# Superblocks 1 and 2 of a fused convolution and squared-ReLU network: casts on ScalarE, maxima a pair a step, 16-bit copies a superblock later

## The chip, the cores and the metric

The kernel runs on one core of one Trainium2 chip. The metric is the device time of one execution in microseconds (us); before the change it is 2076.97 us, the median of three runs (2076.81 to 2077.22).

The core has five instruction queues that run side by side and wait for each other by semaphores: TensorE (PE, its weight loads as PEld), VectorE (DVE), ScalarE (ACT), GpSimd (POOL) and SyncE (SP, which here issues nearly all DMAs). Each queue works strictly in its own order: an instruction that waits holds back all behind it.

## The reference

A causal convolution over seven taps whose weights are a softmax per head, and behind it a two-layer network with the square of a ReLU:

```python
def _attn_ref(x, weight):                    # x: 8 x 4096 x 192, weight: 8 heads x 7 taps
    ...
    w = np.exp(weight - np.max(weight, axis=-1, keepdims=True))
    w = w / (np.sum(w, axis=-1, keepdims=True) + 1e-09)
    ...
    out = np.einsum('hk,bskhg->bshg', w, x_unf)
    return out.reshape(B, S, D).astype(np.float32)

def _moe_ref(x, w_in, w_out, s, b):          # x: 32768 x 192, 2048 hidden columns
    h = x @ w_in
    r = np.maximum(h, 0.0)
    g = s * (r * r) + b
    return (g @ w_out).astype(np.float32)
```

## The kernel before, in words

**Tiling.** The 32768 tokens are cut into 32 superblocks of 1024, and each of these into two blocks j of 512. The 2048 hidden columns are cut into eight pairs p of two chunks of 128. The main loop (from line 981 on) runs over the steps (n, j, p): superblock, block, pair. Superblock 0 has its own code; the loop begins at n = 1. A step calls `first(n, j, p)`: 18 multiplications that put hidden columns of the block into a PSUM tile h (two such tiles exist). ScalarE takes `relu` of h into q and squares q in place. `square` then casts q to a rounded copy qh, and `lows` (or `half_lows` from n = 3 on) subtracts qh from q on VectorE, which gives the low part ql: every factor is split into a high and a low part, so that products of reduced precision add up to full precision. Each step is put into `queue`, and `second(n, j, p, qh, ql)`, which multiplies with the output weights into four accumulators, follows at least two steps later (`LAG = 2`); a block's first pair is held one step longer, since the accumulators must first be evicted by ScalarE (lines 809 and 812) and summed by GpSimd (813, 817, 822). In that place two `first` stand together and then two `second`.

**Tokens.** Superblock n + 1 is convolved during superblock n, a tap at a time: the class `Tokens` holds the work as a generator of 28 steps, first seven taps into accA for block 0 and its split into sA, then seven taps into accB (the last 64 features of both blocks) and its split into tB, then accA for block 1. `convolve(k)` does the next k taps on VectorE, behind what VectorE and ScalarE had been given before. What a call couldn't do, because a part ended, is owed to the next. After a split, `swap` copies sA to wA and tB to wB with the two halves of the partitions exchanged: two DMAs on SyncE each. `first` of the new superblock reads sA, then tB and wB, then wA.

**Scales.** From superblock 3 on ql is 16-bit, and tokens are scaled by powers of two. For that `peak()` takes the maxima of the tokens two superblocks ahead, at step (n, 1, 3). `to_all` sends them to a DRAM tile "there" and back to all partitions as a tile t: two DMAs on SyncE, of which the second waits for the first. `scale()` uses t at step (n, 1, 7). The weights have scales too: `weight_tops` and `weight_peaks` take their maxima in block (2, 0), `weight_scales` computes g, c and c8 with a few small operations on VectorE and GpSimd, `rescale(p)` multiplies the output weights of pair p by g on ScalarE after their last use in superblock 2, and `halve(p)` makes 16-bit copies of their high parts for the products with the 16-bit ql. `biases()` in step (2, 0, 0) computes what b adds to the output and adds it to the three blocks that had been kept back in the output buffers.

**Order.** Instructions are recorded in the order of the code, and a scheduler orders them per engine; `behind(...)` keeps a piece of work behind what an engine had last. DMAs of later loads (xA, xB) are often issued a superblock before the place in the code that asks for them. The words used below: "there" and "t" are the two DMAs of `to_all`, "peak" the two reductions on line 207.

Of the kernel before, what the change touches and what calls it, by code (L numbers as in the profile page):

```python
# [9 lines left out]
F32 = mybir.dt.float32  # L10
# [4 lines left out]
AF = mybir.ActivationFunctionType  # L15
# [18 lines left out]
SCALED = 3  # L34
# [10 lines left out]
def conv_attention_then_squared_relu_mlp(  # L45
# [23 lines left out]
    nc = tc.nc  # L69
    D, T = outT.shape  # L70
    NPAIR = weights64.shape[0]
    K = taps.shape[2]
    PAD = K - 1
    DB = D - P
# [47 lines left out]
    def behind(*engines):  # L122
        return last_of(*engines)()
# [34 lines left out]
    def greatest(wide, count):  # L158

        out = small.tile([P, 2], F32, name="m")[:, 0:count]  # L160
        nc.vector.tensor_reduce(
            out, wide.rearrange("p (c k) -> p c k", c=count), axis=AX.X, op=ALU.max
        )
        return out

    def powers(of, power, other, low):

        nc.vector.tensor_scalar(of, of, 2.0**low, 2.0**60, op0=ALU.max, op1=ALU.min)
        of, power, other = (v.bitcast(I32) for v in (of, power, other))
        nc.vector.tensor_scalar(power, of, EXPONENT, None, op0=ALU.bitwise_and)  # L170
        nc.vector.tensor_scalar(
            other, of, EXPONENT, EXPONENT, op0=ALU.bitwise_and, op1=ALU.bitwise_xor
        )

    g, c, undo, c8 = (scales[:, k : k + 1] for k in range(4))
# [173 lines left out]
    WB = wide_w.tile([P, NPAIR, 2, 2 * DB], F32R, name="WB")  # L349
# [231 lines left out]
    def weight_tops(p):  # L581

        for to, w in (
            (tops[:, p : p + 1], W[:, p, 0, 0:CI]),
            (tops[:, NPAIR + p : NPAIR + p + 1], W[:, p, 0, CI:CB]),
            (tops[:, 2 * NPAIR + p : 2 * NPAIR + p + 1], WB[:, p, :, 0:DB]),
        ):
            nc.vector.tensor_reduce(  # L588
                to, w.bitcast(F32), axis=AX.XY if w.shape[1] == 2 else AX.X, op=ALU.max,
                apply_absolute_value=True,  # L590
            )

    def weight_peaks():

        for k, some in enumerate((tops[:, 0:NPAIR], tops[:, NPAIR:])):
            nc.vector.tensor_reduce(both_tops[:, k : k + 1], some, axis=AX.X, op=ALU.max)
        return to_all(both_tops)

    def weight_scales(wide):

        m = greatest(wide, 2)
        power, other = scales[:, 4:6], scales[:, 6:8]
        powers(m, power, other, -30)
        nc.gpsimd.tensor_scalar(c, other[:, 0:1], 0.5, None, op0=ALU.mult)
        nc.gpsimd.tensor_scalar(c8, other[:, 0:1], 2.0**2, None, op0=ALU.mult)
        nc.gpsimd.tensor_scalar(g, other[:, 1:2], 2.0**3, None, op0=ALU.mult)
        nc.gpsimd.tensor_tensor(undo, power[:, 0:1], power[:, 0:1], op=ALU.mult)
        nc.gpsimd.tensor_scalar(undo, undo, power[:, 1:2], 2.0**-12, op0=ALU.mult, op1=ALU.mult)
        nc.gpsimd.tensor_scalar(undo, undo, sb, None, op0=ALU.mult)

    halves = []

    def halve(p):

        if not halves:
            free = wordp.tile([P, CT, 2], I32, name="words").bitcast(F16)
            free = free.rearrange("p f w -> p (f w)")
            halves.append(free[:, 0 : NF * P].rearrange("p (f c) -> p f c", f=NF))
            halves.append(free[:, NF * P : NF * (P + DB)].rearrange("p (f c) -> p f c", f=NF))
        f = slice(2 * p, 2 * p + 2)  # L620
        a = W[:, p, 0, CI:CB].bitcast(F32).rearrange("p (f c) -> p f c", f=2)
        nc.scalar.activation(halves[0][:, f, :], a, AF.Identity, scale=g)
        nc.scalar.activation(
            halves[1][:, f, :], WB[:, p, :, 0:DB].bitcast(F32), AF.Identity, scale=g
        )

    def rescale(p):

# [23 lines left out]
    def first(n, j, p, meanwhile=None):  # L652
        h = ps_h.tile([P, 2, BLK], F32, name="h")
        halves = [tok[n].half(j, i) for i in range(2)]

        def both(w, part, at, start, stop):

            for i in range(2):
                chunk = halves[i][at]
                rows = slice(i * HB, (i + 1) * HB)  # L660
                nc.tensor.matmul(  # L661
                    h[:, i, :], w_in(w, p, chunk[0], rows), folded(chunk[part]),
                    start=start, stop=stop,
                )

        for at in (0, 2, 1):
            both(0, 1, at, at == 0, False)
            both(0, 2, at, False, False)
            both(1, 1, at, False, at == 1)
            if meanwhile and at == 0:  # L670
                meanwhile()
        return h

    def relu(h, scale=1.0):
        q = act.tile([P, 2, BLK], F32, name="q")
        nc.scalar.activation(q, h, AF.Relu, scale=scale)  # L676
        return q

    def squares(h, cast, scale=1.0):
        return square(relu(h, scale), cast)  # L680

    def square(q, cast):
        nc.scalar.activation(q, q, AF.Square)  # L683
        qh = qs.tile([P, 2, BLK], F32R, name="qh")
        cast(qh, q)  # L685
        return q, qh

    def lows(q, qh):
        ql = qs.tile([P, 2, BLK], F32R, name="ql")
        nc.vector.tensor_tensor(ql, q, qh.bitcast(F32), op=ALU.subtract)  # L690
        return qh, ql
# [188 lines left out]
    def load_tokens(n):  # L880
        if n < NSUP:
            ahead[n] = Tokens(n)
            ahead[n].load()

    def start_tokens(n):
        if n < NSUP:
            if n not in ahead:
                load_tokens(n)
            tok[n] = ahead.pop(n)
# [7 lines left out]
    def convolve(k):  # L897


        k += owed[0]  # L900
        with behind(nc.vector, nc.scalar):
            while k and coming[0] in tok:
                try:
                    stop = next(tok[coming[0]].todo)
                except StopIteration:
                    coming[0] += 1
                    continue
                k -= 1
                if stop:
                    break  # L910
        owed[0] = k if coming[0] in tok else 0
# [54 lines left out]
    for n, j, p in steps:  # L966
        if p == 0:
            tok[n].finish(j)
            if j == 0:
                with headed():  # L970
                    start_tokens(n + 1)
            else:
                tok.pop(n - 1)
                if n >= SCALED:
                    tok[n].unscale()
                    tok_s[n] = tok[n].s
        if j == 1 and SCALED <= n + 2 < NSUP:
            if p == 0:
                load_tokens(n + 2)
            elif p == 3:  # L980
                with behind(nc.vector):
                    ahead[n + 2].peak()
            elif p == 7:
                with behind(nc.vector):
                    ahead[n + 2].scale()
        if n == SCALED - 1:
            if j == 1:
                halve(p)
            elif p < 4:
                with behind(nc.vector):  # L990
                    weight_tops(2 * p)
                    weight_tops(2 * p + 1)
                    if p == 3:
                        wide_tops = weight_peaks()
            elif p == 7:
                with behind(nc.vector):
                    weight_scales(wide_tops)
        with begun() if n == 1 else ExitStack():
            h = first(n, j, p)
            if n < SCALED:  # L1000
                low = lows(*squares(h, nc.vector.tensor_copy))
            else:
                low = half_lows(n, j, p, *squares(h, nc.vector.tensor_copy, c if n == SCALED else 1.0))
            queue.append((n, j, p, *low))
        if (n, j) == (1, 1):
            if p < NPAIR - 1:
                with behind(nc.vector):
                    column_sums(p + 1)
            convolve(1)
        elif p < NPAIR - 1 or n == 1:  # L1010

            convolve(3 if n == 1 else 3 - p % 2 if n == 2 else 2)
        if (n, j, p) == (2, 0, 0):
            biases()


        while queue and len(queue) > LAG + (queue[0][2] == 0 and queue[0][:2] != (1, 0)):
            item = queue.pop(0)
            (second if item[0] else second_whole)(*item)
# [47 lines left out]
```

## Time and profile before

| | |
|---|---|
| median of three runs | 2076.97 us |
| the profiled execution | 2077.24 us |
| its span, first to last instruction | 2075.5 us |
| PE / DVE / ACT / POOL busy | 99% / 89% / 63% / 21% |
| granted TensorE clock | 1.00 |

The page gives each engine's busy time over the span. Beside it three views are used. The view of stretches gives each engine's busy time between two moments. The timeline gives instructions in the order of time, with the idle time before one and what ended it in square brackets. The view of groups collects instructions of one line and shape: count, busy time, the mean of one in ns, and after the bar the idle time before them. The wait view says who waited for whom: us in total, times, longest.

### The profile page before, as it was taken

Reading aid. Unit: us, or ns where it says so; the run is one execution under the profiler, and the core shown is the slowest. Engines: PE = TensorE matmul, PEld = TensorE weight load, DVE = VectorE, ACT = ScalarE, POOL = GpSimd, SP = SyncE. Lnnn points to the kernel's source line nnn. Section 1 sums busy time; section 2 is a strip of 40 time slices with the busy share of each in tenths; the row PEclk is TensorE's granted clock in tenths of the full one; section 3 lists DMA queues with packets and bytes.
Section 4 is the critical chain, followed back from the end, with each engine's and each line's share of the span. In section 5 each row is a group of like instructions: output and inputs, shape, how many; then the busy total and the mean of one; then the engine's idle time right before and its main releaser. Section 6 shows DMA issues by size and latency. Waiting matters only on the chain.

```text
span 2075.5 us, 43142 instructions
## 1 busy us (share of the span) xinstructions
PE 2052.6 (99%) x18404; PEld 1593.7 (77%) x18404; DVE 1842.3 (89%) x2201; ACT 1298.3 (63%) x1440; POOL 429.6 (21%) x298
## 2 busy tenths in 40 slices
PE   9998999999999999999999999999999999999999
PEld 6786777777777777777777777777777777777776
DVE  9998899889988889988899898899888899888975
ACT  8855765666666656656666656666666566566665
POOL 0014221212211212212212112122112122122210
PEclk9999999999999999999999999999999999999999
DMA  5012221212221222221122212222212222221210
GB/s 193 21 50 68 59 60 48 64 50 68 59 60 47 57 57 63 62 56 54 52 62 60 59 48 61 53 69 57 62 47 57 57 62 62 56 55 44 54 42 19
DMA packets 58640, 121.35 MB, mean 58 GB/s; under 512 B 16400, under 2 KB 20496, under 8 KB 58448
## 3 DMA queue, kind: packets, MB, share of 16 engines
q1 hardware_dynamic: 58304, 118.47, 21.0%
q8 instruction: 144, 2.36, 0.5%
q14 instruction: 48, 0.39, 0.1%
q10 hardware_dynamic: 144, 0.13, 0.0%
HBM read 35.57 MB, written 25.20 MB: 29 GB/s over the span
## 4 chain that ended last, share of the span: by engine, by line
PE 91%; DVE 6%; ACT 1%; issue 1%; DMA 0%; POOL 0%; SPq 0%; DVEq 0%; ACTq 0%
PE h L661 45%; PE acc L773 30%; PE acc L792 10%; PE acc L758 5%; DVE ql L690 1%; DVE accA L239 1%; DVE qh L685 1%; DVE c L405 0%; DVE t L391 0%; ACT q L676 0%; DVE tops L588 0%; ACT q L683 0%; DVE W L411 0%; DVE words L571 0%; DVE t L388 0%
## 5 line engine op out<-in xcount | busy, mean ns | idle before, releaser
L676 ACT ACTIVATE q<-h 128x1024 f32<-128x1024 f32 x496 | 506.5, 1021 | 638.7 <-PE h L661 637.1
L703 DVE TENSOR_TENSOR ql<-q,qh 128x1024 f16<-128x1024 f32 x464 | 584.9, 1261 | 24.7 <-PE acc L773 0.9
L683 ACT ACTIVATE q<-q 128x1024 f32<-128x1024 f32 x512 | 542.0, 1059 | 14.2
L773 PE MATMUL acc<-qh,W 64*128 64x512 f32 x3960 | 515.1, 376 | 0.2
L685 DVE CAST qh<-q 128x1024 fp32r<-128x1024 f32 x497 | 349.8, 704 | 167.4 <-ACT q L683 163.9
L661 PE MATMUL h<-sA,W 64*128 64x512 f32 x3072 | 488.3, 423 | 4.7 <-ACT q L676 2.9
L773 PEld LDWEIGHTS acc<-qh,W 64*128 64x128 f32 x3960 | 376.2, 186 | 53.2 <-ACT oA L812 0.8
L661 PE MATMUL h<-wA,W 64*128 64x512 f32 x3072 | 416.1, 376 | 0.0
L661 PE MATMUL h<-wB,W 64*128 64x512 f32 x1536 | 413.8, 376 | 1.3 <-DMA wB<-tB 1.3
L661 PE MATMUL h<-tB,W 64*128 64x512 f32 x1536 | 413.7, 376 | 0.0
L661 PEld LDWEIGHTS h<-sA,W 64*128 64x128 f32 x3072 | 286.5, 186 | 100.8 <-ACT oA L809 23.5
L239 DVE SCALAR_TENSOR_TENSOR accA<-xA,taps,accA 128x512 f32<-128x512 f32 x348 | 341.9, 983 | 6.2
L661 PEld LDWEIGHTS h<-wA,W 64*128 64x128 f32 x3072 | 291.5, 186 | 40.8
L773 PE MATMUL acc<-qh,WB 64*128 64x512 f32 x1980 | 312.9, 388 | 4.4 <-DVE qh L685 2.3
L661 PEld LDWEIGHTS h<-tB,W 64*128 64x128 f32 x1536 | 285.0, 186 | 27.2 <-issue 0.2
L661 PEld LDWEIGHTS h<-wB,W 64*128 64x128 f32 x1536 | 285.0, 186 | 15.6 <-DMA wB<-tB 2.0
L792 PE MATMUL acc<-ql,words 64*128 64x512 f16 x1852 | 280.6, 382 | 0.0
L817 POOL TENSOR_TENSOR oA<-oA,oA 128x512 f32<-128x512 f32 x61 | 111.1, 1821 | 808.0 <-ACT oA L812 808.0
L773 PEld LDWEIGHTS acc<-qh,WB 64*128 64x128 f32 x1980 | 188.9, 186 | 37.9 <-DVE qh L685 3.7
L792 PEld LDWEIGHTS <-words 64*128 64x128 f16 x1852 | 53.8, 95 | 111.0 <-issue 111.0
L239 DVE SCALAR_TENSOR_TENSOR accB<-xB,taps,accB 128x512 f32<-128x512 f32 x174 | 131.2, 754 | 3.1
L822 POOL TENSOR_TENSOR oC<-oC,oB 64x512 f32<-64x512 f32 x60 | 95.9, 1599 | 147.9 <-DMA oC<-oB 140.2
(152 smaller groups left out, 1397.9 us busy)
## 6 DMA issues: line engine op xcount, KB each, us to landing
wA<-sA SPq DMA_DIRECT2D x126, 256.0 KB, 3.7
outT<-oA SPq DMA_DIRECT2D x63, 256.0 KB, 2.0
wB<-tB SPq DMA_DIRECT2D x60, 256.0 KB, 3.2
xA<-in_xA SPq DMA_DIRECT2D x24, 515.0 KB, 4.4
xB<-in_xB SPq DMA_DIRECT2D x32, 259.0 KB, 2.6
oC<-oB SPq DMA_DIRECT2D x61, 128.0 KB, 2.2
outT<-oC SPq DMA_DIRECT2D x60, 128.0 KB, 2.3
words<-in_w SPq DMA_DIRECT2D x7, 768.0 KB, 6.4
```

The lines of the kernel that those rows point to most:

```text
L239: nc.vector.scalar_tensor_tensor(acc, src, w[:, k : k + 1], acc, op0=ALU.mult, op1=ALU.add)
L661: nc.tensor.matmul(h[:, i, :], w_in(w, p, chunk[0], rows), folded(chunk[part]), start=start, stop=stop,)
L676: nc.scalar.activation(q, h, AF.Relu, scale=scale)
L683: nc.scalar.activation(q, q, AF.Square)
L685: cast(qh, q)
L690: nc.vector.tensor_tensor(ql, q, qh.bitcast(F32), op=ALU.subtract)
L703: nc.vector.tensor_tensor(ql.rearrange("p f (b a) -> p f b a", a=2), *(v.rearrange("p f (a b) -> p f b a", a=2) for v in (q, qh.bitcast(F3 ...
L758: nc.tensor.matmul(to[k * DB :][0:DB], halves[1][:, 2 * p + k, :], ql[:, k, :], start=False, stop=p == NPAIR - 1, skip_group_check=True,)
L773: nc.tensor.matmul(accs[to + 2 * i], w(f, r), folded(q[r, f % 2, :]), start=start and f == 0, stop=stop and f == ends[i],)
L792: nc.tensor.matmul(accs[2 * i], halves[0][r, f, :], ql[r, f % 2, :], start=False, stop=f == ends[i],)
L817: nc.gpsimd.tensor_tensor(o[0], o[0], o[2], op=ALU.add)
L822: nc.gpsimd.tensor_tensor(oB, oC, o[1][0:DB], op=ALU.add)
```

## The change

It has five parts. (1) In superblocks 1 and 2 the casts of block (1, 0), of block (2, 0) and of the odd pairs of block (1, 1) run on ScalarE, 20 in all; the others stay on VectorE. (2) The weights' maxima are taken for one pair in each of the eight steps of block (2, 0), and no longer for two pairs in each of its first four. (3) So `weight_peaks` moves from step (2, 0, 3) to (2, 0, 7), and `weight_scales` from (2, 0, 7) to (2, 1, 3). (4) `halve` moves from block (2, 1) to block (3, 0); by then the weights carry g already, so that it copies without a factor. (5) In superblock 2 `convolve` gets two taps after each step, no longer three and two by turns.

```diff
-        nc.scalar.activation(halves[0][:, f, :], a, AF.Identity, scale=g)
-        nc.scalar.activation(
-            halves[1][:, f, :], WB[:, p, :, 0:DB].bitcast(F32), AF.Identity, scale=g
-        )
+        nc.scalar.copy(halves[0][:, f, :], a)
+        nc.scalar.copy(halves[1][:, f, :], WB[:, p, :, 0:DB].bitcast(F32))
...
         if n == SCALED - 1:
-            if j == 1:
-                halve(p)
-            elif p < 4:
+            if j == 0:
                 with behind(nc.vector):
-                    weight_tops(2 * p)
-                    weight_tops(2 * p + 1)
-                    if p == 3:
+                    weight_tops(p)
+                    if p == NPAIR - 1:
                         wide_tops = weight_peaks()
-            elif p == 7:
+            elif p == 3:
                 with behind(nc.vector):
                     weight_scales(wide_tops)
+        elif (n, j) == (SCALED, 0):
+            halve(p)
         with begun() if n == 1 else ExitStack():
             h = first(n, j, p)
             if n < SCALED:
-                low = lows(*squares(h, nc.vector.tensor_copy))
+                on_scalar = (n, j) in ((1, 0), (2, 0)) or (n, j, p % 2) == (1, 1, 1)
+                low = lows(*squares(h, nc.scalar.copy if on_scalar else nc.vector.tensor_copy))
...
-            convolve(3 if n == 1 else 3 - p % 2 if n == 2 else 2)
+            convolve(3 if n == 1 else 2)
```

What this does to the order shows at three places. First VectorE in block (3, 1), whose order repeats in every later superblock; qh is a step's cast, ql its subtraction, accB the taps, tB and hiB the split, peak the maxima two superblocks ahead. Before, from the split after the subtraction of (3, 1, 1):

```order
L267 CAST hiB<-accB 128x512
L271 CAST tB<-accB 64x512
L272 TENSOR_TENSOR tB<-accB,hiB 64x512
L685 CAST qh<-q 128x1024
L703 TENSOR_TENSOR ql<-q,qh 128x1024
L271 CAST tB<-accB 64x512
L272 TENSOR_TENSOR tB<-accB,hiB 64x512
L237 TENSOR_SCALAR accA<-xA,taps 128x512
L207 TENSOR_REDUCE peak<-xA 128x1
L207 TENSOR_REDUCE peak<-xB 128x1
L685 CAST qh<-q 128x1024
L703 TENSOR_TENSOR ql<-q,qh 128x1024
```

Now, from the cast of (3, 1, 2):

```order
L683 CAST qh<-q 128x1024
L701 TENSOR_TENSOR ql<-q,qh 128x1024
L239 SCALAR_TENSOR_TENSOR accB<-xB,taps,accB 128x512 x2
L207 TENSOR_REDUCE peak<-xA 128x1
L207 TENSOR_REDUCE peak<-xB 128x1
L683 CAST qh<-q 128x1024
L701 TENSOR_TENSOR ql<-q,qh 128x1024
L239 SCALAR_TENSOR_TENSOR accB<-xB,taps,accB 128x512
L683 CAST qh<-q 128x1024
L701 TENSOR_TENSOR ql<-q,qh 128x1024
L267 CAST hiB<-accB 128x512
L271 CAST tB<-accB 64x512
```

The split of accB stood ahead of the maxima and stands behind them now, after the subtraction of (3, 1, 4).

Second SyncE's DMAs at the same place: outputs of the block before, the swap of tB into wB, the two DMAs of the maxima, loads. Before:

```order
L821 DMA outT<-oA 128x512
L816 DMA oC<-oB 64x512
L826 DMA outT<-oC 64x512
L248 DMA wB<-tB 64x1024
L247 DMA wB<-tB 64x1024
L151 DMA there<-peak 128x2x1
L153 DMA t<-there 128x256
L198 DMA xA<-in_xA 128x1030
```

Now:

```order
L819 DMA outT<-oA 128x512
L814 DMA oC<-oB 64x512
L824 DMA outT<-oC 64x512
L151 DMA there<-peak 128x2x1
L153 DMA t<-there 128x256
L195 DMA xB<-in_xB 128x518
L248 DMA wB<-tB 64x1024
L247 DMA wB<-tB 64x1024
L198 DMA xA<-in_xA 128x1030
```

The two DMAs that write wB have moved behind "there", "t" and a load of xB (which before stood further ahead).

Third ScalarE in block (2, 1); words are the 16-bit copies, W and WB the output weights, scales holds g. Before, around the relus of (2, 1, 0) and (2, 1, 1):

```order
L622 ACTIVATE words<-W,scales 128x256
L623 ACTIVATE words<-WB,scales 128x128
L622 ACTIVATE words<-W,scales 128x256
L676 ACTIVATE q<-h 128x1024
L623 ACTIVATE words<-WB,scales 128x128
L683 ACTIVATE q<-q 128x1024
```

Now, around the relu of (2, 1, 4) and the one after it:

```order
L628 ACTIVATE W<-W,scales 128x2x256
L622 CAST words<-W 128x256
L674 ACTIVATE q<-h 128x1024
L681 ACTIVATE q<-q 128x1024
L628 ACTIVATE WB<-WB,scales 128x256
L623 CAST words<-WB 128x128
L628 ACTIVATE W<-W,scales 128x2x256
L622 CAST words<-W 128x256
L674 ACTIVATE q<-h 128x1024
L681 ACTIVATE q<-q 128x1024
```

The copies stood ahead of the block's second relu and waited for the scales; each pair's copies now stand beside its rescaling.

## The prediction

> Below, "step (n,j,p)" is superblock n (from 0), block j, hidden pair p; "the second superblock" is n = 1, "the third" n = 2. My forecast: **slower, 2169 us**. The change wins back some 14 us in n = 1 and n = 2, and then pays about 3.9 us at 27 later superblock borders.
>
> **What bounds the kernel now.** I read the page first, then a table of stretches of the run, then TensorE's own timeline and its waits.
>
> ```profile
> span 2075.5 us, 43142 instructions
> PE 2052.6 (99%) x18404; PEld 1593.7 (77%) x18404; DVE 1842.3 (89%) x2201; ACT 1298.3 (63%) x1440; POOL 429.6 (21%) x298
> ...
> 120.52:154.43 33.91, 33.13 (x308) 28.62 (x305) 32.81 (x44) 18.79 (x21) 5.46 (x3) 1.00 0.14 38
> 154.43:196.27 41.84, 35.56 (x315) 29.38 (x312) 39.69 (x71) 18.31 (x22) 19.80 (x12) 1.00 0.27 77
> 196.27:238.23 41.96, 35.71 (x306) 28.35 (x304) 30.96 (x41) 29.84 (x48) 6.06 (x10) 1.00 0.21 50
> 238.23:2012.00 1773.77, 1773.77 (x16212) 1374.29 (x16210) 1595.88 (x1853) 1101.78 (x1193) 387.81 (x259) 1.00 0.21 57
> ```
>
> The columns of the last four rows are the stretch, its length, then busy time of PE, PEld, DVE, ACT and POOL, the granted clock, DMA share and GB/s. From 238 us on TensorE is never idle: there is nothing to gain there, and every new wait of TensorE is paid in full. The time that can be won lies before 238 us. How much, I take from the starts of steps:
>
> ```profile
> 116.42 0.38 PE L661 MATMUL h<-sA,W 64*128 64x512 f32 x2
> 120.52 0.38 PE L661 MATMUL h<-sA,W 64*128 64x512 f32 x2
> 154.43 0.38 PE L661 MATMUL h<-sA,W 64*128 64x512 f32 x2
> 196.27 0.38 PE L661 MATMUL h<-sA,W 64*128 64x512 f32 x2
> 238.23 0.38 PE L661 MATMUL h<-sA,W 64*128 64x512 f32 x2
> ...
> PE acc L773 <- DVE ql L690: 5.6, 6, 1.9
> PE acc L773 <- DVE qh L685: 2.3, 3, 0.8
> PE acc L773 <- ACT oB L809: 2.0, 1, 2.0
> PE h L661 <- DMA wB<-tB: 1.3, 2, 0.7
> ...
> L642 PE MATMUL h<-bb,words 64*128 64x1 f32 x8 | 0.5, 226 | 0.0
> ```
>
> An undisturbed step takes 120.52 - 116.42 = 4.10 us (38 multiplications in 19 side-by-side pairs, 0.216 us a pair), so eight take 32.8. The blocks (1,1), (2,0), (2,1) took 33.9, 41.8 and 42.0: 1.1, 9.0 and 9.2 too much. Block (1,0), whose first steps have no second product yet, lost about 0.9 to late ql. Together **20.2 us** are lost, of which 0.5 are the eight small products for the bias (last row), that stay. (The four rows of waits, 90 to 240 us, add up to less, because a product that waits for its operands is also drawn longer.) The 9.0 us of (2,0) I divide so: 2.0 for wB at its start (worked out in part 4), 0.5 for the bias, 3.0 for the eviction of oB (the 2.0 of its row and about 1 of slow products behind it), and the rest, 3.5, late qh and ql.
>
> **Part 1: twenty casts to ScalarE.** The prices, from rows of the first superblocks:
>
> ```profile
> L690 DVE TENSOR_TENSOR ql<-q,qh 128x1024 fp32r<-128x1024 f32 x8 | 9.8, 1225 | 0.5
> L239 DVE SCALAR_TENSOR_TENSOR accA<-xA,tap,accA 128x512 f32<-128x512 f32 x12 | 9.0, 750 | 0.3
> L685 DVE CAST qh<-q 128x1024 fp32r<-128x1024 f32 x8 | 5.5, 689 | 1.9 <-ACT q L683 1.9
> ...
> L676 ACT ACTIVATE q<-h 128x1024 f32<-128x1024 f32 x16 | 16.3, 1016 | 0.4 <-PE h L661 0.2
> L685 ACT CAST qh<-q 128x1024 fp32r<-128x1024 f32 x15 | 15.7, 1048 | 0.5
> ...
> L812 ACT ACTIVATE oB<-acc,sb 128x512 f32<-128x512 f32 x4 | 2.7, 676 | 0.0
> ```
>
> In (1,0) VectorE does per step a cast, a subtraction and three taps: 0.69 + 1.23 + 3 x 0.75 = 4.17 us against TensorE's 4.10, so it falls behind and stays behind. Without the cast it is 3.48. ScalarE then does relu, square and cast, three times about 1.03, 3.1 us a step, inside 4.10. So the late ql of n = 1 go, but for the first step, where nothing hides that ScalarE's cast is 0.36 longer: of the 2.0 us of n = 1, 0.6 stay. In (2,0) the casts (8 x 0.69) and half of each maxima step go from VectorE's worst stretch: of the 3.5 us of late qh and ql I leave 0.5. ScalarE also evicts four accumulators a block between these casts (0.68 each, last row) and casts two tiles sA as large: 8 x 3.1 + 6 x 0.68 = 28.9, still under 32.8.
>
> **Part 2: the maxima, a pair a step.** Their number stays; the bias of (2,0,0) no longer stands behind two pairs of them. VectorE being ahead too, the bias comes about 3 us sooner relative to TensorE, the GpSimd additions behind it free the output buffer sooner, and the wait for the eviction of oB (3.0 us) shrinks to about 0.7.
>
> **Part 3: the 16-bit copies a superblock later.** In (2,1) ScalarE now stands still for the scales, and then has 16 copies between its relus:
>
> ```profile
> L622 ACT ACTIVATE words<-W,scales 128x256 f16<-128x256 f32 x8 | 4.0, 496 | 6.2 <-POOL scales L606 6.2
> ```
>
> That is a wait of 6.2 us and 4.0 us of copies, their eight smaller partners on top, and TensorE's late relu, qh and ql of (2,1) follow from it. After the change the copies stand beside the rescaling, under 1 us a step, on an engine that then is busy for nearly the whole 4.10. The scales come at step 3 and their GpSimd steps behind that block's output additions; a relu is late by about 3 us there, of 4 us that the lag of two steps allows. I leave 1.0 of the 9.2 us.
>
> Still there in n = 2: the wait for wB in (2,0,0), 2.0 before and about 1.6 after (both sides move forward by 1.5 to 2 us), and a new one of about 1.4 into (3,0,0), priced like the next part. Left in all: 0.6 + 0.5 + 0.7 + 1.0 + 1.6 + 1.4 + 0.5 = 6.3. **Gain 20.2 - 6.3 = 14 us**, between 8 (half of what I call gone stays) and 18.
>
> **Part 4: where the taps now stand.** The last line of the diff (two taps a step in n = 2, not three and two by turns) looks harmless, but it shifts the taps against the steps, and the shift stays for all later superblocks. So accB's taps end after the maxima of the tokens two superblocks on (peak), not before; hence in SyncE's queue the swap of tB into wB now stands behind "there", "t" and an xB load. The trace of before has this very order once, in n = 1, and shows its price:
>
> ```profile
> 149.75 0.34 SPq L153 DMA_DIRECT2D t<-there  x1
> 150.19 0.47 SPq L248 DMA_DIRECT2D wB<-tB  x1
> ...
> 157.75 0.59 PE L661 MATMUL h<-wA,W 64*128 64x512 f32 x4
> ```
>
> "t" can't be issued before "there" has landed, and wB lands late behind the broadcast "t". The products with wA should have come 12 multiplications (1.30 us) after 154.43, at 155.73; they came at 157.75, so TensorE lost 2.02 us with "t" issued at 149.75. In other words: **loss = issue of t + 6.7 - start of the next superblock** (149.75 + 6.7 - 154.43 = 2.0).
>
> In the steady part, before the change:
>
> ```profile
> 405.97 0.38 PE L661 MATMUL h<-sA,W 64*128 64x512 f32 x2
> 425.94 0.57 PE L661 MATMUL h<-sA,W 64*128 64x512 f32 x2
> ...
> 412.40 0.55 SPq L248 DMA_DIRECT2D wB<-tB  x1
> 415.08 0.38 SPq L151 DMA_DIRECT2D there<-peak  x1
> 423.04 0.33 SPq L153 DMA_DIRECT2D t<-there  x1
> ...
> wB<-tB SPq DMA_DIRECT2D x56, 256.0 KB, 3.2
> xB<-in_xB SPq DMA_DIRECT2D x26, 259.0 KB, 2.6
> ```
>
> Step (5,1,3) starts at 405.97, superblock 6 at 425.94; wB left at 412.4, long before. "there" to "t" is 423.04 - 415.08 = 7.96 us. When does peak end after the change? By the new order it stands behind the casts and subtractions of (5,1,0) to (5,1,2) and four taps of accB:
>
> ```profile
> 403.75 1.25 DVE L703 TENSOR_TENSOR ql<-q,qh 128x1024 f16<-128x1024 f32 x1
> ...
> 407.23 1.07 ACT L683 ACTIVATE q<-q 128x1024 f32<-128x1024 f32 x1
> ...
> 404.31 1.83 POOL L817 TENSOR_TENSOR oA<-oA,oA 128x512 f32<-128x512 f32 x1 [24.30 <-ACT oA L812]
> ...
> 409.93 1.86 POOL L822 TENSOR_TENSOR oC<-oC,oB 64x512 f32<-64x512 f32 x1 [2.36 <-DMA oC<-oB]
> ...
> 373.40 3.46 DVE L239 SCALAR_TENSOR_TENSOR accA<-xA,taps,accA 128x512 f32<-128x512 f32 x2
> ...
> 413.23 1.22 DVE L207 TENSOR_REDUCE peak<-xA 128x1 f32<-128x1030 f32 x1
> 414.37 0.68 DVE L207 TENSOR_REDUCE peak<-xB 128x1 f32<-128x518 f32 x1
> ```
>
> The subtraction of (5,1,1) gives VectorE back at 404.9. Two taps beside GpSimd's additions (as at 373.40, 3.46) end at 408.3, when the square of (5,1,2) is just done. Cast and subtraction end at 410.3; two taps, the first beside GpSimd's next addition (1.7), the other 0.75, at 412.7; peak (1.74) at 414.4. So "t" goes at 414.45 + 7.96 = 422.4, and the loss is 422.4 + 6.7 - 425.94 = 3.2 us, plus what the xB load between t and wB adds: between nothing and its 2.6 us. I take 0.7, near the lower end, since its set-up runs beside that of t, which is issued only 0.4 us ahead. **3.9 us a border**. Taps without a neighbour on GpSimd would bring peak 0.9 us earlier and the loss to 2.3; above I take 5.0. It happens wherever a peak is taken in the steady part, n = 3 to 29: 27 borders, **105 us** (62 to 135). Nothing covers it, since TensorE was never idle there, and a wait at one border leaves the next border's distances as they were.
>
> **The sum**, against the profiled execution's own 2077.24 us (span 2075.5 and 1.7 around it; the median of the three runs is 2076.97): 2077.2 - 14 + 105.3 = 2168.5, say 2169.
>
> **A rule of the Trainium skill beside it.** The steady wB row says 3.2 us from issue to landing, the one wB behind a "t" took some 6. "DMA: Bandwidth & Descriptors", section "Anatomy of one DMA", gives for a transfer issued by GpSimd about 2.0 us plus its bytes at 436 GB/s, whatever is ahead of it: as an estimate by that page 2.6 us for wB's 256 KB, so no wait in the steady part and some 2063 us. Its section "Two DMAs through the same engine are not ordered" says that descriptors of one queue start in order, which is the other answer. The row of n = 1 decides for me.
>
> **The rivals.** (a) *wB isn't held up*: with no queue ahead it lands 3.2 us after an issue at about 423.9, at 427.1; its products come 0.9 us after 425.94, at 426.8. That leaves at most 0.5 us a border: 2077 - 14 + 27 x (0 to 0.5) = 2063 to 2077. This is the one that ends faster; it decides from a landing within 3.0 us of the second issue. Against it: 157.75. For it: only one such case is in the trace. (b) *ScalarE becomes the bound* in n = 1 and 2: casts wait behind an eviction that waits for the bias, and the 14 us are not gained: 2077 + 105 = 2182. For it: ScalarE would be at 28.9 of 32.8 us there. (c) *The change doesn't relieve VectorE*, since its subtraction must now wait for ScalarE: same time as (b). (d) *The border costs more*: the whole xB load counts, 27 x 5.8 = 157: 2220.
>
> **How the numbers follow.** Forecast 0.68, (b) and (c) together 0.11, (d) 0.06, (a) 0.15 (two thirds of it faster, the rest near the old time). 0.2% is 4.2 us, about what a measurement can tell from no change. Slower 0.85, same 0.05, faster 0.10. The range, from 2077 - 18 + 62 = 2121 to 2077 - 8 + 135 = 2204, I stretch a little downwards, to 2105, since the landing behind the broadcast rests on one case.
>
> **What would show it.** In the changed profile TensorE should wait for the DMA of wB about 27 times more, 3 to 5 us each, right at the superblock's start; SyncE should show t, xB, wB, wB in this order; before 240 us the waits for ql, qh and q should nearly vanish, and step (3,0,0) start near 223. I am wrong if wB lands within 3 us of its issue, or if peak ends less than 5 us into step (n,1,3).

## The result and the profile after

The changed kernel takes **2250.75 us** (median of five runs, 2248.64 to 2255.14), against 2076.97 us for the kernel before, also over five (2076.72 to 2078.02). The ratio is 1.0837, with a 95% interval from 1.0822 to 1.0852: 8.4% slower. The forecast was 2169 us with a range up to 2204, so the direction and the place were right and the size was not: the border costs 6.6 us where 3.9 were forecast. The profiled execution took 2248.72 us. One of the eight executions of the first experiment's first kernel took 2670.23 us, at a granted clock of 0.75, and its ratio leaves that one out.

The page of the changed kernel: span, busy time, the clock's slices, the costliest group of wB, and the landing of its DMA.

```profile
span 2246.9 us, 43117 instructions
PE 2128.6 (95%) x18404; PEld 1637.6 (73%) x18404; DVE 1797.2 (80%) x2181; ACT 1316.7 (59%) x1460; POOL 381.4 (17%) x298
...
PEclk9999999999999999999999999999999999999999
...
L659 PE MATMUL h<-wB,W 64*128 64x512 f32 x1536 | 439.2, 391 | 104.8 <-DMA wB<-tB 104.7
...
wB<-tB SPq DMA_DIRECT2D x60, 256.0 KB, 7.1
```

TensorE now waits, and nearly all its idle time was ended by the DMA of wB, which takes 7.1 us from issue to landing and took 3.2. But the idle time is 105 us, and the kernel lost 171.5. TensorE's busy time grew too, from 2052.6 to 2128.6 us, for the same 18404 multiplications. The row of the clock shows nothing of this: a slice is 56 us long, and a 9 stands for everything from 0.9 up. So the next view is the one of stretches, first over the whole steady part, then around one border (superblock 6 begins at 429.63). The columns are the stretch, its length, busy time of PE, PEld, DVE, ACT and POOL, the granted clock, DMA share and GB/s.

```profile
238.00:2110.00 1872.00, 1768.56 (x15472) 1350.74 (x15470) 1499.43 (x1779) 1048.60 (x1135) 328.99 (x248) 0.97 0.21 52
...
422.00:429.60 7.60, 7.60 (x72) 6.03 (x72) 7.41 (x12) 4.39 (x5) 0.00 (x0) 1.00 0.01 5
429.60:434.00 4.40, 1.26 (x12) 0.78 (x8) 4.26 (x9) 0.80 (x1) 1.32 (x2) 0.99 0.81 201
434.00:437.40 3.40, 3.24 (x13) 2.26 (x15) 0.55 (x1) 0.00 (x0) 0.96 (x2) 0.50 0.02 5
437.40:440.30 2.90, 2.90 (x18) 1.73 (x16) 0.67 (x1) 2.08 (x2) 0.00 (x0) 0.50 0.00 0
```

After the wait the granted clock is 0.50 for at least 6.3 us. TensorE's timeline at the same border, with two rows of the step before for comparison:

```profile
427.43 0.81 PE L659 MATMUL h<-wA,W 64*128 64x512 f32 x6
428.08 0.59 PE L771 MATMUL acc<-qh,WB 64*128 64x512 f32 x4
...
429.63 1.00 PE L659 MATMUL h<-sA,W 64*128 64x512 f32 x6
430.47 0.38 PE L659 MATMUL h<-tB,W 64*128 64x512 f32 x1
433.98 0.79 PE L659 MATMUL h<-wB,W 64*128 64x512 f32 x1 [3.14 <-DMA wB<-tB]
434.94 0.79 PE L659 MATMUL h<-wB,W 64*128 64x512 f32 x1 [0.16 <-DMA wB<-tB]
...
435.95 1.49 PE L659 MATMUL h<-wA,W 64*128 64x512 f32 x6
437.23 1.06 PE L771 MATMUL acc<-qh,WB 64*128 64x512 f32 x4
```

From the six products with wA to the next group took 428.08 - 427.43 = 0.65 us before the border and 437.23 - 435.95 = 1.28 behind it. So each border costs twice: the second wB product comes 434.94 - 429.63 = 5.31 us after the start, not 1.05, and the rest of the step runs at half speed. Over the 27 borders (starts of the superblocks 4 to 30) step (n,0,0) is 6.59 us longer on average: **4.54 us** by which the second wB product is late, and **2.05 us** beyond that, nearly all of it half clock, as the third experiment shows. 27 x 6.59 = 178 us; the early part gives 8.0 back (superblock 4 starts at 291.9, and started at 299.9); together 170 of the 171.5 us.

SyncE's queue shows the order that had been read from the program; in VectorE's rows tB is finished before t has been issued:

```profile
418.32 0.38 SPq L151 DMA_DIRECT2D there<-peak  x1
426.01 0.33 SPq L153 DMA_DIRECT2D t<-there  x1
426.44 0.38 SPq L195 DMA_DIRECT2D xB<-in_xB  x1
426.91 0.47 SPq L248 DMA_DIRECT2D wB<-tB  x1
427.47 0.55 SPq L247 DMA_DIRECT2D wB<-tB  x1
...
424.64 0.69 DVE L272 TENSOR_TENSOR tB<-accB,hiB 64x512 fp32r<-64x512 f32 x1
```

The rows of the stretches add that the DMA engines move hardly anything up to the border (share 0.01 until 429.60), though t was issued at 426.01, and are then busy at a share of 0.81 until 434.00.

### The profile page after: what moved, and what is told of

Its sections match the earlier page's. It is cut to its first block, busy times and chain, and to the rows that moved or that the text cites. A ratio compares the mean times of both kernels' runs of the same rounds, so it can differ in the third digit from the quotient of the medians.

```text
span 2246.9 us, 43117 instructions
## 1 busy us (share of the span) xinstructions
PE 2128.6 (95%) x18404; PEld 1637.6 (73%) x18404; DVE 1797.2 (80%) x2181; ACT 1316.7 (59%) x1460; POOL 381.4 (17%) x298
## 4 chain that ended last, share of the span: by engine, by line
PE 63%; DVE 20%; DMA 9%; ACT 4%; issue 4%; DVEq 0%; POOL 0%; SPq 0%
PE h L659 31%; PE acc L771 20%; DMA wB<-tB 9%; PE acc L790 6%; PE acc L756 5%; DVE ql L701 5%; DVE qh L683 3%; DVE accB L239 3%; DVE peak L207 2%; DVE tB L272 2%; ACT q L681 2%; ACT q L674 2%; DVE ql L688 1%; DVE tB L271 1%; DVE hiB L267 1%
## 5 line engine op out<-in xcount | busy, mean ns | idle before, releaser
L683 DVE CAST qh<-q 128x1024 fp32r<-128x1024 f32 x477 | 331.4, 695 | 383.1 <-ACT q L681 377.1
L659 PE MATMUL h<-wB,W 64*128 64x512 f32 x1536 | 439.2, 391 | 104.8 <-DMA wB<-tB 104.7
L771 PE MATMUL acc<-qh,W 64*128 64x512 f32 x3960 | 528.1, 383 | 0.8 <-ACT oA L810 0.7
L659 PE MATMUL h<-wA,W 64*128 64x512 f32 x3072 | 435.6, 390 | 0.0
L659 PE MATMUL h<-tB,W 64*128 64x512 f32 x1536 | 433.5, 387 | 0.0
L771 PEld LDWEIGHTS acc<-qh,W 64*128 64x128 f32 x3960 | 387.0, 192 | 59.5 <-ACT oA L810 1.0
L659 PEld LDWEIGHTS h<-wA,W 64*128 64x128 f32 x3072 | 304.0, 194 | 45.9
L771 PE MATMUL acc<-qh,WB 64*128 64x512 f32 x1980 | 324.5, 401 | 0.0
L239 DVE SCALAR_TENSOR_TENSOR accA<-xA,taps,accA 128x512 f32<-128x512 f32 x348 | 306.5, 881 | 6.1
L239 DVE SCALAR_TENSOR_TENSOR accB<-xB,taps,accB 128x512 f32<-128x512 f32 x174 | 215.9, 1241 | 3.1
```

The lines of the kernel that those rows point to most:

```text
L239: nc.vector.scalar_tensor_tensor(acc, src, w[:, k : k + 1], acc, op0=ALU.mult, op1=ALU.add)
L659: nc.tensor.matmul(h[:, i, :], w_in(w, p, chunk[0], rows), folded(chunk[part]), start=start, stop=stop,)
L771: nc.tensor.matmul(accs[to + 2 * i], w(f, r), folded(q[r, f % 2, :]), start=start and f == 0, stop=stop and f == ends[i],)
```

## The experiments

**1. The taps' line: undone, and alone.** The first kernel is the changed one with the old line back, the second the kernel before with only the new line:

```diff
-            convolve(3 if n == 1 else 2)
+            convolve(3 if n == 1 else 3 - p % 2 if n == 2 else 2)
```

> The changed kernel with only its last line undone (three and two taps by turns in superblock 2). Theory S (the shift of the taps puts the swap of tB behind the maxima's two DMAs, and the half clock after each wait does the rest): no wait for wB at the 27 later borders, clock 1.00 from 240 us on, 2077 - 8 = about 2069 us, which keeps the 8 us that the changed kernel won before superblock 4. Rival R (casts on ScalarE or the late 16-bit copies cost the time): stays near 2250 us.

> The kernel before with only that last line. Theory S: 27 borders of about 6.6 us each, 2077 + 179 = about 2256 us, clock about 0.97. Rival R: 2077 us within a few us.

Measured: undone 2072.57 us, ratio to before 0.9974 (0.9964 to 0.9985). Every superblock from the fourth on takes 63.04 us again, and no border waits. Alone 2279.7 us, ratio 1.0975 (1.0958 to 1.0992): all 27 borders are longer, by 7.27 us each, and run at half clock. That is 24 us more than expected: a border costs 0.7 us more than in the changed kernel, and superblock 4 starts 3.7 us later than before. So this one line is the whole loss, and the other four parts together are a gain of 0.26%. That gain is smaller than the 14 us of the forecast, and the first kernel's trace shows one reason, in ScalarE's and GpSimd's timelines in (2,1):

```profile
214.09 0.72 ACT L628 ACTIVATE W<-W,scales 128x512 fp32r<-128x512 f32 x1 [9.70 <-POOL scales L606]
...
212.27 0.70 POOL L607 TENSOR_TENSOR scales<-scales 128x1 f32<-128x1 f32 x1 [3.01 <-DVE scales L171]
...
PE h L659 <- ACT q L674: 4.0, 1, 4.0
PE h L659 <- DMA wB<-tB: 2.7, 2, 2.1
```

ScalarE stands still for 9.70 us until g is there, all its relus wait behind, and TensorE waits 4.0 us for one: steps (2,1,5) and (2,1,6) take 8.3 and 7.0 us.

**2. Is it the place of wB's issue behind t?** Three kernels move t against wB: t a step earlier, t a step later, and the load of xB out of the way. In the first two the number of the step is the only edit:

```diff
-            elif p == 3:
+            elif p == 2:
                 with behind(nc.vector):
                     ahead[n + 2].peak()
```

(and `p == (3 if n < SCALED else 4)` for the later one); in the third

```diff
-                load_tokens(n + 2)
+                with behind(nc.sync):
+                    load_tokens(n + 2)
```

> The changed kernel with the loads of xB and xA held to their own superblock, so that no xB load stands between t and wB. Theory S: wB lands 0.7 us sooner or a little more, idle about 3.0 us a border instead of 3.8; if the clock still falls each time, 2250 - 27 x 0.8 = about 2230 us; if so short a wait keeps the clock, 27 x 3.1: about 2155 us. Rival Q (wB is late because the queue ahead of it holds an xB load as large as itself, not for t): the wait all but goes, about 2100 us or less.

> The changed kernel with peak (and the round trip behind it) at step 4 of the second block instead of step 3, from the fourth superblock's tokens on. Theory: t is issued about 3.7 us later, so the second wB lands some 3 to 3.7 us later at each border (the load of xB now stands ahead of the round trip): 27 x 3.0 to 3.7 = 80 to 100 us more, 2330 to 2350, and up to 2400 if a second half-clock stretch follows at every border. Rival (wB is late for a reason of its own, its engines or tB): 2240 to 2260.

> The changed kernel, with the maxima of the block after next (peak, and the round trip there -> t behind it) put at step 2 of the second block instead of step 3. Theory: peak ends about 3.9 us earlier, so t is issued 7.3 us before the next superblock instead of 3.4; by the formula (issue of t + 6.7 - start) the loss is below zero, wB then waits for tB alone, and the time is about 2072 (2062 to 2085), like the kernel with the taps line undone. Rival (the place of tB's split on VectorE, not SyncE's order, makes wB late): no change, 2240 to 2255. If the loads of xA and xB have not landed at step 2, VectorE waits for them there: 2085 to 2200.

Measured: xB out of the way 2203.99 us, ratio 1.0612 (1.0598 to 1.0627); later 2304.64, 1.1087 (1.107 to 1.1104); earlier 2092.16, 1.0068 (1.0054 to 1.0082). Means over the 27 borders, worked out from the traces (issue of t and of the second DMA of wB against the superblock's start; delay of the second wB product against the 1.05 us of an undisturbed step; half clock within the 14 us from the start; what step (n,0,0) lost):

| kernel | t issued | wB issued | delay | half clock | lost | lost - delay |
|---|---|---|---|---|---|---|
| peak earlier | -7.46 | -3.73 | 0.91 | 0 | 1.01 | 0.10 |
| changed kernel | -3.38 | -1.82 | 4.54 | 4.80 | 6.59 | 2.05 |
| xB not between | -3.05 | -2.02 | 3.30 | 3.03 | 4.85 | 1.55 |
| peak later | -0.44 | 0.92 | 5.77 | 6.83 | 8.51 | 2.74 |

With peak later the load of xB moved ahead of the round trip as well, as SyncE's rows show, so its order is that of the kernel with xB out of the way:

```profile
427.98 0.34 SPq L195 DMA_DIRECT2D xB<-in_xB  x1
429.72 0.38 SPq L151 DMA_DIRECT2D there<-peak  x1
438.06 0.32 SPq L153 DMA_DIRECT2D t<-there  x1
438.47 0.47 SPq L248 DMA_DIRECT2D wB<-tB  x1
```

Between these two t moves by 2.61 us and the wB product by 2.47: wB follows the issue of t, as the formula says. Its constant is 3.30 + 3.05 = 6.35 and 5.77 + 0.44 = 6.21. The 6.7 of n = 1 had been read at the first product with wA; at the second wB product, which came at 157.22, the same case gives 157.22 - 1.05 - 149.75 = 6.42, so the constant held; and xB between t and wB costs 4.54 + 3.38 - 6.35 = 1.6 us, where 0.7 had been taken. The expectation for the later peak missed that xB would move. The earlier peak falls short of its 2072 us: t goes at 411.04, but tB is not finished before 414.30, xB is still loaded between the two, and wB is late once more, by 0.9 us:

```profile
411.04 0.33 SPq L153 DMA_DIRECT2D t<-there  x1
412.05 0.54 SPq L195 DMA_DIRECT2D xB<-in_xB  x1
414.32 0.47 SPq L247 DMA_DIRECT2D wB<-tB  x1
...
413.61 0.69 DVE L272 TENSOR_TENSOR tB<-accB,hiB 64x512 fp32r<-64x512 f32 x1
...
PE h L659 <- DMA wB<-tB: 13.8, 28, 0.9
...
wB<-tB SPq DMA_DIRECT2D x56, 256.0 KB, 5.8
```

The issue of wB now waits for tB, but its landing still takes 5.8 us, not 3.2: on average t lands 1.19 and xB 0.01 us before the border, the two halves of wB 0.94 and 1.89 us after it. By those 3.2 us the second, issued at 414.32, would land at 417.5 as an estimate, ahead of the border at 418.79. So the taps' line puts wB behind t and xB, and it makes tB later as well; that the later tB costs time by itself is not shown.

**3. Is the rest the clock?** The changed kernel, with work for TensorE in the wait: six products with sA, which are there already, repeated five times as groups of their own ahead of each border's first step.

```diff
+        if n > SCALED and (j, p) == (0, 0):
+            for _ in range(5):
+                both(0, 1, 0, True, False)
+                both(0, 2, 0, False, False)
+                both(1, 1, 0, False, True)
         for at in (0, 2, 1):
```

> The changed kernel, but at each border from superblock 4 on TensorE repeats its first six products five times more (30 products, 3.25 us at full clock), so that it computes while wB is on its way; wB itself comes no sooner. Theory S: 3.8 us of each border are the wait, and 2.8 are products at half clock behind an idle TensorE; with the idle time filled the clock stays at 1.00 and the border costs 4.0 instead of 6.6: 2250 - 27 x 2.6 = about 2180 us. Rival C (the products behind the wait are slow for another reason, say DMAs that read the same memory): slow products stay, about 2250 us or, if the repeats are paid in full, up to 2340 us.

Measured: 2213.18 us, ratio 1.0648 (1.063 to 1.0666): 37.6 us less than the changed kernel, with 840 multiplications more. The same border, TensorE's timeline and the stretches around it:

```profile
429.71 4.24 PE L659 MATMUL h<-sA,W 64*128 64x512 f32 x36
433.79 0.38 PE L659 MATMUL h<-tB,W 64*128 64x512 f32 x1
434.64 0.48 PE L659 MATMUL h<-wB,W 64*128 64x512 f32 x1 [0.47 <-DMA wB<-tB]
435.62 0.48 PE L659 MATMUL h<-wB,W 64*128 64x512 f32 x1 [0.51 <-DMA wB<-tB]
...
429.70:435.60 5.90, 4.94 (x42) 3.77 (x38) 4.86 (x9) 0.78 (x1) 2.30 (x3) 1.00 0.76 154
435.60:439.50 3.90, 3.88 (x36) 3.15 (x38) 0.34 (x1) 2.08 (x2) 0.00 (x0) 1.00 0.00 0
```

wB comes no sooner (5.98 us after the start on average, 5.59 in the changed kernel), but the clock stays at 1.00 here and at 23 of the 27 borders. The time is 33 us above the expected 2180: the second wB product is 4.93 us late, where 3.8 us of idle time had been counted, and four borders are half-clocked after all. Sorting the borders of all these kernels by the half-clocked time that follows gives what it costs. Without any, the loss exceeds the delay by 0.11 us (23 borders here, 3 of the kernel without xB between). With one stretch of 3.41 us it exceeds it by 1.67 to 1.74 (the changed kernel's 16, 24 without xB, 4 here), half of 3.41. With two, 6.83 us, by 2.61 to 2.74 (11 of the changed kernel, 27 with peak later), less than half of 6.83: there the half clock begins while TensorE still waits. So the second part of the loss is the clock, and it is shown from both sides: keep the wait and fill it, and the clock's share goes at 23 of 27 borders; shorten the delay to 3.30 us, and it stays at 24 of 27.

Which waits cost it can be worked out from the traces. In each of the 14 traces of this document all half-clocked stretches begin at whole multiples of 3.413 us from the first one (146 stretches, within 0.01 us). Take the pieces of this grid that ran at full clock, from 95 us after the start to 30 us before the end. All 123 in which TensorE was busy for less than 0.425 of the time were followed by half clock, none of the 7933 with more than 0.56 was, and six of the 14 between. Two borders of the kernel with xB out of the way, for each the piece with most of its wait and the next one:

```profile
432.26:435.67 3.41, 2.09 (x15) 1.62 (x17) 2.45 (x6) 0.22 (x1) 2.29 (x3) 1.00 0.16 38
435.67:439.08 3.41, 3.41 (x34) 2.73 (x32) 1.45 (x2) 1.86 (x2) 0.00 (x0) 1.00 0.00 0
...
1992.15:1995.56 3.41, 1.14 (x6) 0.48 (x5) 3.27 (x8) 0.00 (x0) 1.24 (x2) 1.00 0.54 129
1995.56:1998.97 3.41, 3.41 (x18) 2.68 (x17) 0.63 (x1) 1.39 (x2) 1.05 (x2) 0.50 0.00 0
```

At the first TensorE waited 1.98 and 0.55 us, but the grid parts the wait: it was busy for 2.20 us of the piece before and for 2.09 of this one, and the clock stayed. At the second it waited less, 1.72 and 0.55 us, but all in one piece with 1.14 us busy, and the clock fell. So whether a short wait costs the clock depends on where it falls.

**4. wB on another queue.** The changed kernel, with the two DMAs of wB on ScalarE's queue from the third superblock's tokens on:

```diff
-        def swap(self, to, of):
+        def swap(self, to, of, j=0):
...
-            nc.sync.dma_start(to[0:HB], of[HB:P])
-            nc.sync.dma_start(to[HB:P], of[0:HB])
+            e = nc.scalar if of.shape[1] == 2 and self.n > 1 and j is None else nc.sync
+            e.dma_start(to[0:HB], of[HB:P])
+            e.dma_start(to[HB:P], of[0:HB])
...
-                    self.swap(self.wB, self.tB)
+                    self.swap(self.wB, self.tB, None)
```

> The changed kernel, with the two DMAs wB<-tB issued on ScalarE's queue instead of SyncE's for every superblock from the third on; the taps and all else stay as changed. Theory (wB is late because its issue stands behind that of t on SyncE, and t waits for the round trip of the maxima): tB is written 0.7 us before t is issued, so with the queue left the wait goes, the 27 borders fall from 10.27 to 3.7-4 us, no half clock is left at them, and the time falls by 27 x 6.6 = 178 us to about 2072 (2062 to 2085). Rival (the DMA engines are busy with the round trip and the load of xB at that time, or tB itself is late): wB lands as late as now, 2200 to 2250. Between them, if ScalarE, which must wait for tB before it can issue, holds up its relus: 2100 to 2200.

Measured: 2113.43 us, ratio 1.0179 (1.0163 to 1.0195). The border's step is 0.09 us longer than before, no half clock follows, and the waits for wB come to 1.2 us in all; but the case between came true. ScalarE must wait for tB before it can issue, and the relu behind it is late:

```profile
484.05 1.56 ACTq L248 DMA_DIRECT2D wB<-tB  x1
484.71 0.33 SPq L153 DMA_DIRECT2D t<-there  x1
485.66 1.02 ACT L675 ACTIVATE q<-h 128x1024 f32<-128x1024 f32 x1 [7.63 <-issue]
...
PE h L660 <- ACT q L675: 23.7, 25, 2.7
```

Superblocks 4 to 29 take 63.9 to 67.0 us instead of 63.04. Data, transfers and their sizes are the same, and at most borders wB now goes ahead of t and is in time. But the rows show one of five borders (superblocks 7, 9, 11, 13 and 28) at which the issue of ScalarE's second DMA of wB ended only after that of t, and there it landed 6.0 to 6.4 us after the end of its issue, on a queue of its own, against 2.8 to 4.4 us at the others whose landing is in the trace. So it is the order, wB behind t, that makes wB late, on either queue; what of t holds it is not shown. About 1 us of the time that wB gains is this stall itself, as it delays the border.

**5. The early part.** Two kernels split the other four parts: the casts alone (kernel before with `on_scalar` and nothing else), and maxima, scales and copies alone (changed kernel with all casts on VectorE and the old taps' line).

> The kernel before with only the 20 casts moved to ScalarE: maxima two pairs a step, scales at step 7 of (2,0), 16-bit copies in (2,1) and the taps line as before. Theory (the casts relieve VectorE in (1,0), (1,1) and (2,0), and the scales are in time for ScalarE): steps of (2,0) and of (1,1) are shortened, no stall for g beyond that of before: 2066 to 2073. Rival (VectorE's two maxima a step still set (2,0), the casts bring nothing): 2074 to 2078.

> The changed kernel without its 20 casts on ScalarE and with the old line of taps: of the change only the maxima a pair a step, the scales at step 3 of (2,1) and the 16-bit copies a superblock later are left. Theory (the casts give most of the early gain, and the late scales hold up ScalarE before the 16-bit product): the early part loses about as much at (2,1,5) and (2,1,6) as the spread maxima give back in (2,0), 2072 to 2082. Rival (the casts on ScalarE bring nothing, the spread maxima all): 2069 to 2073, as with the casts.

Measured: casts alone 2075.82 us, ratio 0.9992 (0.9983 to 1.0001); the rest alone 2078.0, ratio 1.0004 (0.9994 to 1.0013). Neither differs measurably from before, while both together gave 2072.57. At the start of superblock 4 their traces are 2.0 us ahead and 0.4 us behind (counted from the start of superblock 1), and 6.9 us ahead with both. With the casts alone the steps of (2,0) after the first fall to their undisturbed lengths (6.3 us for (2,0,3), which was 9.3), but (2,0,0) takes 9.6, and (2,1,0), (2,1,1) and (2,1,3) take 7.3, 7.0 and 10.8: ScalarE waits 7.62 us for g at 197, as the copies stand there still. The number is the rival's; its reason (the maxima would still set (2,0)) isn't what the trace shows.

Then three kernels on the scales' place, the taps' line undone in all. The first only moves `weight_scales` from step 3 to step 1 of (2,1):

> The changed kernel with the line of taps undone, and the weights' scales made at step 1 of (2,1) instead of step 3. Theory (ScalarE waits 9.7 us for the scale g there, and with the scales earlier the stall of TensorE at (2,1,5) and (2,1,6) goes): steps of 8.3 and 7.0 us become about 4, so 5 to 8 us less than with the line of taps undone alone: about 2066 (2063 to 2069). Rival (the rescaling itself is too much work for ScalarE there, whenever it begins): 2071 to 2074.

Measured: 2074.89 us, ratio 0.9987 (0.9978 to 0.9996), worse than at step 3. VectorE itself now waits for the round trip of the weights' maxima:

```profile
207.21 0.42 DVE L161 TENSOR_REDUCE m<-t 128x2 f32<-128x256 f32 x1 [7.40 <-DMA t<-there]
...
208.76 0.48 PE L771 MATMUL acc<-qh,WB 64*128 64x512 f32 x2 [3.10 <-DVE qh L683]
```

The cast qh stands behind that wait, and step (2,1,3) takes 12.69 us, half clock included. The next kernel takes step 2, and in n = 1 also takes peak a step earlier, against wB behind t in (2,0,0); the last takes two pairs' maxima in step 0 of (2,0), so that the round trip starts a step sooner.

```diff
-            elif p == 3:
+            elif p == (2 if n == 1 else 3):
                 with behind(nc.vector):
                     ahead[n + 2].peak()
...
-            elif p == 3:
+            elif p == 2:
                 with behind(nc.vector):
                     weight_scales(wide_tops)
```

> The changed kernel with the line of taps undone, the weights' scales at step 2 of (2,1), and the maxima of the third superblock (peak in (1,1)) at step 2 instead of 3. Theory: with the taps undone, (2,0,0) still takes 7.97 us for wB behind t, which falls to about 4.6 as it did with peak at step 2 everywhere; g comes 5 us earlier, so (2,1,5) and (2,1,6) fall from 15.3 to 8.5 to 11 us, and VectorE waits at most 1.5 us for the round trip of the weights' maxima: 2072.6 less 3.4 less 4 to 6, plus up to 2 given back at (2,0,3): about 2066 (2062 to 2070). Rival (at step 2 VectorE still waits for the round trip and holds up qh as at step 1): 2070 to 2075.

> As the kernel before it in this call, with the weights' maxima of the first two pairs both taken at step 0 of (2,0), so that the last pair's stand at step 6 and the round trip there begins about 4 us earlier. Theory: the scales at step 2 then wait for nothing, 1 to 4 us less than that kernel, about 2064. Rival (the extra maximum at step 0 makes the squares late there, or the release of t, not the maxima, sets the round trip): the same or 1 to 3 us more.

Measured: **2066.86 us**, ratio 0.995 (0.9938 to 0.9963), and 2066.57, ratio 0.9948 (0.9936 to 0.9961). Both beat the kernel before and the changed one. In the first, (2,0,0) takes 4.55 us, and (2,1,4), (2,1,5) and (2,1,6) take 5.4, 6.1 and 4.1 (4.1, 8.3 and 7.0 with the line of taps undone alone), though (2,0,3) takes 8.6 and no longer 6.3. What TensorE waits for in 90 to 240 us:

```profile
PE acc L771 <- DVE ql L688: 2.1, 3, 0.8
PE acc L771 <- ACT oB L810: 1.6, 1, 1.6
PE acc L771 <- DVE qh L683: 0.7, 1, 0.7
PE acc L771 <- ACT oA L807: 0.2, 1, 0.2
```

The last kernel shortens (2,1,4) and (2,1,5) to 4.10 and 4.85 and gives it back at (2,0,3), which takes 10.8: no gain, as its rival said.

## Why the prediction was wrong in size

**Part 4, the border: right in mechanism, short by a term.** "Loss = issue of t + 6.7 - start of next superblock" is the right form, at the right 27 borders. Peak was forecast to end 414.4 - 405.97 = 8.4 us into step (n,1,3) and ends at 8.62; the round trip was 7.96 and is 7.69 in the rows above, 7.94 on average; t went 3.38 us ahead of the superblock, forecast 425.94 - 422.4 = 3.5. The constant 6.7 was 0.35 above the 6.35 of the second experiment, most of it because it counts up to the first product with wA. The 0.7 for the load of xB, chosen "since its set-up runs beside that of t", was 0.9 too low: the wB product came 4.54 us late, for a forecast 3.9, 17 us over 27 borders. What is missing altogether is the clock: the sum counted a wait as idle time and nothing more, though each border's wait was followed by 3.41 or 6.83 us at half clock, 2.05 us a border (of which 0.11 are there without half clock too), 55 us in all. The kernel before hardly showed it, as its granted clock was 1.00 in every stretch quoted; the one case the formula came from, a wait of 1.3 us in two pieces at the start of (2,0,0), was not followed by it.

The Trainium skill describes this, in "TensorE: Matmul & The Clock Gate", section "Part 1: The HAM clock gate (the "warmup" mystery)": after an idle window of about 3.4 us TensorE's clock is halved until it has been busy for about as long, by a window of 3413 ns that runs freely. The stretches of 3.41 and 6.83 us and the grid that they begin on agree with it to the digit. Its bound for idle gaps, over some 3.4 us, does not: with xB out of the way 24 of 27 borders were half-clocked, one of them (at 1994.23 and 1995.27 in that trace) after waits of 1.72 and 0.55 us with one product between. It was enough that TensorE was busy for less than some 0.43 of a piece of the grid.

**Parts 1 to 3, the early gain: 8.0 us, not 14.** Of the 8.0 us, 0.3 lie ahead of superblock 1, where the kernels do the same work. Step (3,0,0) starts at 228.7, not near 223. The late ql and qh are gone as forecast, with block (1,0) keeping 0.7 us (forecast 0.6), and the wait for oB in (2,0,3) is wholly gone (0.7 forecast as left). What failed is the 1.0 us left for (2,1): "a relu is late by about 3 us there, of 4 us that the lag of two steps allows". ScalarE waits far longer for g:

```profile
214.49 0.72 ACT L628 ACTIVATE W<-W,scales 128x512 fp32r<-128x512 f32 x1 [8.98 <-POOL scales L606]
...
218.73 1.54 PE L659 MATMUL h<-sA,W 64*128 64x512 f32 x6 [3.32 <-ACT q L674]
```

Steps (2,1,5) and (2,1,6) lose 5.3 us, half clock included. The wait for wB in (2,0,0) had been left at 1.6 us; the step takes 9.12 us, 4.6 more than the 4.55 it takes when wB is in time, again with a half-clocked stretch behind 1.58 and 0.57 us of waiting. The 1.4 us forecast into (3,0,0) aren't there, but (3,0,3), where an eviction stands behind the moved copies on ScalarE, is 1.4 us longer.

**The sum with the measured terms:** 2077.2 - 8.0 + 27 x 6.59 = 2247, against 2248.7. **The rivals:** (a), wB not held up, is out: 7.1 us to land, not 3.2. (b) and (c), no early gain, are out, since the parts without the taps' line gain 4 to 5 us in time. (d), the whole load of xB, was nearest in time by accident: xB costs 1.6 us, not 2.6.

## What to carry to other kernels

Where TensorE is never idle, price a new wait at its length and then the half-clocked stretch behind it, here 1.7 us for one stretch of 3.41. It is lost where TensorE is idle for more than about half of a 3.41 us piece of the grid that runs through the whole execution: waits of 1.72 + 0.55 us lost it at one border, and 2.10 + 0.58 us, in (2,0,0) of the kernel with the taps' line undone, did not. Read the clock in a stretch of a few us, since slices of the page average it away. And a change in how many steps a generator advances moves every DMA that it issues for the rest of the program: compare each queue's order in the steady part before trusting an edit of the start-up. Where an engine has to wait for a round trip, its place must be late enough that this wait is over and early enough for its readers; here both step 1 and step 3 stalled TensorE, and step 2 did much less.

## What the runs showed of the hardware that had not been expected

- Half clock comes in stretches of 3.41 us or twice that, on a grid of 3.41 us, behind a piece of the grid in which TensorE was busy for less than 0.43 of the time (123 of 123; 6 of 14 from there to 0.56, none above). Waits of 1.72 + 0.55 us were enough where they fell into one piece. With xB out of the way, a delay of 3.1 us without it cost 3.2 us, and one of 3.3 us with it 5.1.
- More work can be faster: 840 more multiplications in the wait took 37.6 us off.
- "there" to t took 7.7 to 8.3 us for 1 KB in all of the rows above, and wB of 256 KB landed 3.2 us after its issue with nothing ahead of it, 7.1 us behind t and xB, 6.2 us behind t alone. On ScalarE's queue it was no faster once t had been issued first: 6.0 to 6.4 us from the end of its issue.
